# Long convolution and spectral mixing: even classes enter the modes of the middle pairs by gathered rows of U, with other room counts and an earlier last pair

## The chip, the cores and the metric

The kernel runs on one core of a Trainium2 chip. The metric is the device time of one execution in microseconds. TensorE (PE) multiplies matrices into PSUM, eight banks of 512 32-bit columns; VectorE (DVE) and ScalarE (ACT) copy results out of PSUM and work elementwise; SyncE (SP) and GpSimd (POOL) issue DMA transfers, each into a queue of its own; 16 DMA engines move the bytes.

## The reference

x is [8, 5696, 128], h is [5696, 128]. First a causal long convolution of each batch with h, by transforms of twice the length; then a mixing in the lowest 64 frequencies of the result, a residual and a small product:

```
y  = irfft(rfft(x, 2S) * rfft(h, 2S))[:, :S, :]          # S = 5696
Y  = rfft(y, S); 64 modes m:  Y2[m] = Y[m] (w_r[m] + i w_i[m])
u  = y + irfft(Y2, S)
out = u + max(u @ w_ch, 0)                               # float32
```

## The kernel before

**Stages.** S is 89 x 64, so the transform of length 2S is done in two steps. Step one (a_tile, 32 tiles) transforms over the 89 for each of 64 positions and gives 90 *classes* k = 0 to 89 (frequencies modulo 178, with their mirror images). Step two (second) transforms the 64 positions inside a class, with the twiddle factors in the strip M; the result, 64 complex frequencies as 128 partitions, lies in PSUM. It is multiplied by the filter's spectrum Hs and by its swapped copy (products), which gives U, in float16: two real factors r, two batches b, four classes of 128 channels. Two products with the constants W1 and W2 turn U back from frequencies to positions and give Z. Z goes to a scratch tensor zscr in DRAM, from which the last stage reads it with the classes on the partitions.

**Modes.** The 64 mixing modes are sums over all classes. For each class k and batch of a pair, one product with Z as the stationary operand and a slice of the constant G as the moving one adds to bank 7 (MB, lines 660 to 673): 128 columns for an odd class, but 2 or 4 for an even class, since an even class meets only the modes k/2 and 89 - k/2. At the end of a pair the sums are copied into XT (lines 696 to 699), the second copy with the sign turned.

**Pairs and ticks.** The eight batches are done as four pairs g_ (line 687). A pair has 23 ticks of four classes (NT = 23, the last of two), in three steps that overlap: tick t does second and products for its own classes, the Z products, their two copies by ScalarE and the store for tick t - 2 (LC), and the mode products for tick t - 3 (LM). Pair 0 also makes the filter's spectrum (filter_tick), whose halves are copied across partitions by SP (Hs<-Hs). While a pair runs, GpSimd loads x of the next pair (x_load, at ticks 2, 4, ... 16) and VectorE places it (x_place, ticks 9 to 22). Then comes the *border*: tiles 6 to 31 of the next pair's a_tile, four PSUM slots in turn, copied out by VectorE and ScalarE in turn. After pair 3 comes the last stage: mix multiplies the modes by the weights W, and for each 16 positions Z is loaded as ZT (load_zt, five rooms), turned into y with the constant S4, added to the mixed part (constant IB), multiplied by w_ch and stored.

**What sets the order.** The program is written out by hand: a Recorder keeps one list for each engine, in the order of the calls, and adds a semaphore wait wherever a token ("u", i), ("zs", i, b), ("bank", i) and so on was last written or read elsewhere. Each engine runs its list in order; so does each queue's issuer. A room of a buffer is a token: the writer of a room waits for all who have read it, transfers included.

**Names and lines that the prediction uses.** u_s, the U rooms: three (NU, line 229), room t % 3. z_s, the Z rooms: 6 in pair 0, 10 in pairs 1 and 2, 8 in pair 3 (NZS, line 230). products is line 586, its vector product line 607 (and 599 for the first tick); copied, the copy Xs by ScalarE that three of four products read, line 557; the Z copies and the other plain copies show as line 308 on ScalarE and 312 on VectorE, the scaled ones as 310 and 314; all matmuls are line 320, all transfers line 317. early (line 529) holds the last pair's loads by tick.

Of the kernel before, what the change touches and what calls it, by code (L numbers as in the profile page):

```python
# [4 lines left out]
P = 128  # L5
F16 = mybir.dt.float16
# [117 lines left out]
def bass_long_conv_fft__then__afno_spectral_mix_kernel(nc, x, h, moe_w_r, moe_w_i, moe_w_ch, out):  # L124
# [12 lines left out]

    qq = np.arange(NQ)
    pp = np.arange(J)
    kk = np.arange(NK)  # L140
    fwd = np.exp(-2j * np.pi * np.outer(qq, kk) / (2 * NQ))
    f1 = np.zeros((P, 2 * NK))
    f1[0:NQ] = np.stack([fwd.real, fwd.imag], axis=2).reshape(NQ, 2 * NK)
    mat = np.exp(-2j * np.pi * (pp[:, None, None] * kk[None, :, None] / L + pp[:, None, None] * pp[None, None, :] / J))
# [5 lines left out]
    th = 2.0 * np.pi * np.outer(pp, pp) / J  # L150
    c, s = np.cos(th), np.sin(th)
    w1 = np.block([[c, s], [-c, -s]])
    w2 = np.block([[-s, c], [-s, c]])
# [25 lines left out]
    for k in range(0, NK, 2):  # L179
# [2 lines left out]
        ge += [g[:, k, ri * M + m] for m in ms for ri in range(2)]  # L182
        at_e += 2 * len(ms)
    assert at_e == P
    g = np.concatenate([np.stack(ge, axis=1)] + [g[:, k] for k in range(1, NK, 2)], axis=1)

    def const(name, a):
        return nc.inline_tensor(np.ascontiguousarray(a.astype(np.float16)), name=name)
# [5 lines left out]
    c_ib = const("cIB", ib.reshape(P, -1)[:, 0:SH])  # L194
    c_sg = nc.inline_tensor(np.ascontiguousarray(sg.astype(np.float32)), name="cSG")
    c_g = const("cG", g)
    wd = nc.dram_tensor("wscr", [P, 2 * M * D], F16, kind="Internal")
    zs = nc.dram_tensor("zscr", [NP * NK * P, 2 * D], F16, kind="Internal")

# [26 lines left out]
    a_g = take(HW * 2)  # L226
    g_sb = at("G", GW, F16, a_g)
    ah_sb = at("Ah", HW, F16, a_g)
    NU, NXS, NZ, NZX = 3, 2, 6, 10
    NZS = [NZ] + [NZX] * (NP - 2) + [8]  # L230
    NZL = NZS[-1]
    a_st = take((2 * NU + NXS + NZ) * 2048)
    h_in = at("Hin", J * D, F16, a_st)
# [8 lines left out]
    u_s = [at(f"U{i}", 2048, F16, a_st + i * 4096) for i in range(NU)]  # L242
# [4 lines left out]
    wc_sb = at("Wc", 2 * P, F16, take(2 * P * 2))  # L247
    sg_sb = at("SG", 3, F32, take(12))
    XTW = 3 * M
    xt = at("XT", B * XTW, F16, a_g + GW * 2 + 2048 * (NZX - NZ))  # L250
    assert GW * 2 + 2048 * (NZX - NZ) + B * XTW * 2 <= HW * 2

    ZB = 16
    NC = 5
# [38 lines left out]
    for name, n in (("c", 16), ("x", 26), ("z", 8), ("w", 16), ("t", 10), ("s", 8), ("o", 12), ("p", 16), ("q", 10)):  # L293
        R.ring(name, n)

    def bank(i):
# [197 lines left out]
    ZY = [("zs", i, b) for i in range(NZL, NZX) for b in range(2)]  # L494
# [27 lines left out]
    def load_s4(part):  # L522
# [3 lines left out]

    V, A = "vector", "scalar"
    border = {NT - 1: [(0, 0, V)], NT: [(1, 2, V), (2, 0, V)], NT + 1: [(3, 2, A), (4, 0, V)], NT + 2: [(5, 2, V)]}
    early = {0: lambda: load_id(), 1: lambda: load_w(0), 3: lambda: load_w(1), 6: lambda: load_w(2), 8: lambda: load_w(3),
             12: lambda: load_s4(1), 16: lambda: load_s4(0),  # L530
             14: lambda: clear_zt(0),
             15: lambda: load_zt(0, "gpsimd"),
             NT - 2: lambda: (load_ib(), load_zt(1, "gpsimd", SLACK), load_zt(2, "gpsimd"), clear_zt(1), clear_zt(2))}
    pace = []
    SLACK = [("zd", NP - 1, s_) for s_ in range(NT - NZL)]

# [49 lines left out]
    def products(g_, t, sl):  # L586
        n = len(ticks[t])
        bk = [bank(sl), bank(sl + 1)]
        i = t % NU
        hv = bass.AP(h_sb, KT * t * D, [[2 * HW, P], [HW, 2], [0, 2], [1, n * D]])  # L590
        uv = bass.AP(u_s[i], 0, [[2048, P], [1024, 2], [512, 2], [1, n * D]])
        src = pv(sl, 0, [[0, 2], [512, 2], [1, n * D]])
        if t == 0:
            e = turns("e", list(range(NXS)))
            evac(bass.AP(x_s[e], 512, [[1024, P], [1, n * D]]), pv(sl + 1, 0, [[1, n * D]]), [bank(sl + 1)], [("xs", e)], eng="scalar")
            hv = bass.AP(h_sb, 0, [[2 * HW, P], [HW, 2], [1, n * D]])
            for b, s_, tok in ((0, pv(sl, 0, [[0, 2], [1, n * D]]), bank(sl)),
                               (1, bass.AP(x_s[e], 512, [[1024, P], [0, 2], [1, n * D]]), ("xs", e))):
# [8 lines left out]
        R.add("vector", lambda e: e.tensor_tensor(uv, src, hv, MULT),  # L607
              bk + [("h", t, 0), ("h", t, 1, 0), ("h", t, 1, J)], [("u", i)])

    Z_OLD = [("ag", k) for k in range(NS, NS + 8 * (NZX - NZ))]  # L610
    XPLACE = [9, 10, 12, 15, 16, 18, 20, 22], [9, 10, 13, 14, 17, 18, 20, 22]

    def zroom(g_, s_):
# [1 line left out]

    def xtok(n):
        return [("xt", n, p_) for p_ in range(2)]

    def tick(g_, t):
        if g_ + 1 < NP:  # L620
# [16 lines left out]
            a_tile(j, [sl], e)  # L637
        if g_ + 1 < NP and t % 2 == 0 and 0 < t <= 4 * XC:
            i = t // 2 - 1
            x_load(g_ + 1, i, x_st[i], xtok(i), [("u", t % NU)] + AST)  # L640
        if LC <= t < NT + LC:
            s_ = t - LC
            n = len(ticks[s_])
            i, zi = s_ % NU, zroom(g_, s_)
            zb = [turns("z", ZBANK) for b in range(2)]
            for b in range(2):
                for r in range(2):
                    mm(pv(zb[b], 0, [[1, n * D]]), (W1, W2)[r], u_s[i][:, r * 1024 + b * 512:r * 1024 + b * 512 + n * D],
                       r == 0, r == 1, [("u", i), ("wc",)], [bank(zb[b])])
                evac(bass.AP(z_s[zi], b * D, [[1024, P], [2 * D, n], [1, D]]),  # L650
                     pv(zb[b], 0, [[D, n], [1, D]]), [bank(zb[b])], [("zs", zi, b)], eng="scalar",
                     after=once(("zx", zi, b), Z_OLD) if zi >= NZ else ())
            zo = (g_ * NK + KT * s_) * P * 256
            dma("sync", bass.AP(zs, zo, [[256, P], [P * 256, n], [1, 256]]),
                bass.AP(z_s[zi], 0, [[1024, P], [256, n], [1, 256]]), "z",
                [("zs", zi, 0), ("zs", zi, 1)], [("zd", g_, s_)])
# [30 lines left out]
    for g_ in range(NP):  # L687
        for t in range(NT + LM):
# [7 lines left out]
        evac(bass.AP(xt, 2 * g_ * XTW + M, [[B * XTW, P], [XTW, 2], [1, P]]), pv(MB, 0, [[P, 2], [1, P]]),  # L696
             [bank(MB)], [("xt", g_)], 1.0 / 64, eng="scalar", after=[("ag", k) for k in range(NS + 2 * XN, NK)])
        evac(bass.AP(xt, 2 * g_ * XTW, [[B * XTW, P], [XTW, 2], [1, M]]), pv(MB, M, [[P, 2], [1, M]]),
             [bank(MB)], [("xtn", g_)], -1.0 / 64, eng="vector" if g_ + 1 == NP else "scalar", after=[("ag", k) for k in range(NS + 2 * XN, NK)])
# [197 lines left out]
```

## Time and profile before

| | |
|---|---|
| times of three runs | 392.68, 392.70, 393.31 us; median 392.7 |
| the profiled execution's own time, and its span | 392.87 us; 390.6 us |
| busy share of the span | PE 93%, PEld (weight loads) 72%, DVE 77%, ACT 80%, POOL 22% |
| to the end of pair 0's border | 0 to 109.3 us |
| pair 1: ticks, border | 109.3 to 152.0, 152.0 to 164.8 us |
| pair 2: ticks, border | 164.8 to 208.0, 208.0 to 220.9 us |
| pair 3 | 220.9 to about 262 us |
| last stage | to 390.6 us |
| chain that ended last | PE 63%, DMA 15%, DVE 8%, ACT 6% |

The profile is of one execution. Busy times count the instructions of an engine; a wait is put down to the instruction or transfer that ended it. A row of the timeline is: start, length, engine, line, operation, out<-in, and how many instructions stand in it. The window row gives for a stretch each engine's busy time and number of instructions, the granted share of TensorE's clock, the share of time in which the 16 DMA engines had packets, and the bytes moved. A transfer's time to landing runs from its issue to the last of its semaphore's updates.

### The profile page before, as it was taken

The numbers are of one execution on the slowest core, as the hardware profiler recorded it, in microseconds if no ns is written. First come the engines' busy times: TensorE is split into PE (matmuls) and PEld (weight loads), VectorE is DVE, ScalarE is ACT, GpSimd is POOL, SyncE is SP. The second block draws the span as 40 slices with busy tenths as digits, with TensorE's granted clock in tenths as the row PEclk, the third lists the DMA queues.
The fourth block names the chain that finished last, engine by engine and source line by source line (L and its number), as shares of the span: only waits on it lengthen the run. The fifth ranks groups of instructions, "written<-read, shape, count | busy, mean of one in ns | idle before, by whom it ended". The sixth has DMA issues, their size and how long they took to land.

```text
span 390.6 us, 12485 instructions
## 1 busy us (share of the span) xinstructions
PE 364.1 (93%) x5346; PEld 281.3 (72%) x5346; DVE 301.9 (77%) x346; ACT 311.2 (80%) x489; POOL 85.6 (22%) x134
## 2 busy tenths in 40 slices
PE   7799899998989999999989899989989999999992
PEld 7698766665866667856657666658878988988871
DVE  3369889987998998989998988754437767677784
ACT  8289689997989997899997899984447676777783
POOL 8600022210643210823213210319200000000000
PEclk9899999999999999999999999996999999999998
DMA  7998569998899995999995689999999999998766
GB/s 146 178 283 337 138 126 297 274 251 251 92 135 201 238 268 169 127 136 231 245 261 111 64 264 351 298 354 379 406 388 393 414 407 412 410 399 356 305 274 273
DMA packets 87090, 103.94 MB, mean 266 GB/s; under 512 B 22824, under 2 KB 72616, under 8 KB 83564
## 3 DMA queue, kind: packets, MB, share of 16 engines
q1 hardware_dynamic: 62523, 67.73, 49.7%
q0 software_dynamic: 24512, 35.43, 43.6%
q8 instruction: 42, 0.69, 0.7%
q14 instruction: 13, 0.10, 0.1%
HBM read 70.61 MB, written 51.12 MB: 312 GB/s over the span
## 4 chain that ended last, share of the span: by engine, by line
PE 63%; DMA 15%; DVE 8%; ACT 6%; issue 3%; POOL 3%; SPq 0%; POOLq 0%; DVEq 0%
PE ps L320 63%; DMA ZT4b<-zscr 4%; DMA zscr<-Zt 3%; DMA Hs<-Hs 3%; DMA Hin<-in_h_dram 3%; DMA Xt<-in_x_dram 2%; DVE As L314 2%; DVE U L599 2%; ACT As L310 2%; DVE U L607 1%; DVE Xin L361 1%; ACT UT L308 1%; ACT Zs L308 1%; DVE Hs L312 1%; ACT Xs L308 1%
## 5 line engine op out<-in xcount | busy, mean ns | idle before, releaser
L607 DVE TENSOR_TENSOR U<-Xs,Hs 128x2048 f16<-128x2048 f16 (+1 forms) x73 | 86.9, 1192 | 15.1 <-ACT Xs L308 11.0
L320 PE MATMUL ps<-U,Wc 128*128 128x512 f16 (+1 forms) x368 | 94.0, 376 | 1.3 <-DVE U L607 0.8
L308 ACT CAST Xs<-ps 128x1024 f16<-128x1024 f32 (+1 forms) x77 | 74.7, 974 | 11.9 <-PE ps L320 6.8
L308 ACT CAST Zs<-ps 128x512 f16<-128x512 f32 (+1 forms) x134 | 70.6, 595 | 2.7 <-PE ps L320 2.4
L832 DVE TENSOR_TENSOR O<-ps,R 128x512 f32<-128x512 f32 x81 | 52.5, 685 | 19.8 <-ACT R L831 12.5
L831 ACT ACTIVATE R<-ps 128x512 f32<-128x512 f32 x96 | 50.9, 572 | 16.3 <-PE ps L320 15.8
L314 DVE TENSOR_SCALAR As<-ps 128x720 f16<-128x720 f32 x70 | 57.7, 884 | 5.4 <-PE ps L320 4.8
L320 PE MATMUL ps<-F,Xin 128*128 128x180 f16 x512 | 53.7, 249 | 3.6 <-DVE Xin L361 2.3
L320 PE MATMUL ps<-As,M 64*128 64x128 f16 x1440 | 50.5, 217 | 3.5 <-DVE U L599 2.9
L320 PEld LDWEIGHTS ps<-F,Xin 128*128 128x128 f16 x512 | 44.4, 155 | 12.1 <-DVE Xin L361 2.8
L320 PE MATMUL ps<-WI,UT 128*128 128x256 f16 x360 | 51.8, 279 | 0.5 <-DVE O L832 0.4
L320 PEld LDWEIGHTS ps<-U,Wc 128*128 128x128 f16 x368 | 28.7, 97 | 30.3 <-ACT Zs L308 4.4
L310 ACT ACTIVATE As<-ps 128x720 f16<-128x720 f32 (+1 forms) x61 | 45.7, 770 | 5.7 <-PE ps L320 4.3
L317 POOL DMA_DIRECT2D Xt<-in_x_dram x48 | 26.0, 546 | 101.0 <-PE ps L320 97.1
L320 PEld LDWEIGHTS ps<-As,M 64*128 64x128 f16 x1440 | 40.6, 94 | 9.9 <-DVE U L599 3.6
L308 ACT CAST UT<-ps 128x712 f16<-128x712 f32 x40 | 30.0, 752 | 18.7 <-PE ps L320 17.7
L320 PEld LDWEIGHTS ps<-WI,UT 128*128 128x128 f16 x360 | 39.3, 152 | 4.2 <-issue 1.9
L320 PE MATMUL ps<-IBs,C 128*128 128x356 f16 x128 | 40.5, 326 | 0.6
L320 PEld LDWEIGHTS ps<-G,Zs 128*128 128x128 f16 x524 | 26.6, 96 | 14.9 <-ACT Zs L308 2.2
L607 DVE TENSOR_TENSOR U<-ps,Hs 128x2048 f16<-128x2048 f32 x15 | 34.3, 2283 | 0.0
L320 PE MATMUL ps<-G,Zs 128*128 128x128 f16 (+2 forms) x524 | 33.0, 192 | 0.1
L312 DVE CAST UT<-ps 128x712 f16<-128x712 f32 x24 | 21.4, 890 | 11.0 <-PE ps L320 11.0
(87 smaller groups left out, 509.8 us busy)
## 6 DMA issues: line engine op xcount, KB each, us to landing
out_dram<-O SPq DMA_DIRECT2D x39, 512.0 KB, 8.7
zscr<-Zs SPq DMA_DIRECT2D x64, 256.0 KB, 7.4
Xt<-in_x_dram POOLq DMA_DIRECT2D x24, 320.0 KB, 7.3
zscr<-Zt SPq DMA_DIRECT2D x24, 256.0 KB, 7.3
W<-wscr POOLq DMA_DIRECT2D x4, 1024.0 KB, 9.1
M<-cM POOLq DMA_DIRECT2D x5, 720.0 KB, 20.6
ZT0a<-zscr SPq DMA_DIRECT2D x3, 1024.0 KB, 13.1
Hs<-Hs SPq DMA_DIRECT2D x44, 64.0 KB, 6.3
```

The source lines that it names most:

```text
L308: R.add(e, lambda h_: h_.copy(dst, src), reads, writes, after=after)
L310: R.add(e, lambda h_: h_.activation(dst, src, COPY, scale=scale), reads, writes, after=after)
L312: R.add(e, lambda h_: h_.tensor_copy(dst, src), reads, writes, after=after)
L314: R.add(e, lambda h_: h_.tensor_scalar_mul(dst, src, scale), reads, writes, after=after)
L317: R.add(eng, lambda h_: h_.dma_start(dst, src), reads, writes, ring=ring, after=after)
L320: R.add("tensor", lambda h_: h_.matmul(o, l, r, start=st, stop=sp), reads, writes)
L361: R.add("vector", lambda e: e.tensor_copy(bass.AP(x_sb, i * XN * XS, [[XW, NQ], [XS, XN], [1, D]]), src), list(toks) + XZ, [("xin", i)])
L599: R.add("vector", lambda e, b=b, s_=s_: e.tensor_tensor(bass.AP(u_s[i], b * 512, [[2048, P], [1024, 2], [1, n * D]]), s_, hv, MULT), [tok, ...
L607: R.add("vector", lambda e: e.tensor_tensor(uv, src, hv, MULT), bk + [("h", t, 0), ("h", t, 1, 0), ("h", t, 1, J)], [("u", i)])
L831: R.add("scalar", lambda e: e.activation(rv, src_r, RELU), bk, [("r", i % NR)], after=once(("r", i % NR), G_ALL + XTT + [("y", 0), ("y", 1 ...
L832: R.add("vector", lambda e: e.tensor_tensor(ov, src_u, rv, ADD), bk + [("r", i % NR)], [key + (h_,)], after=once(key, old))
```

## The change

- The frequencies inside a class are put in another order: 32 and 63 change places in the strip M and in W1 and W2. With that, the frequencies that the modes of an even class need stand on partitions 0 and 64 (ticks 0 to 12) or 0, 32, 64 and 96 (ticks 13 to 22) of U.
- In pairs 1 and 2 the mode products of the even classes are left out. Instead, SP copies those partitions of each tick's U to a DRAM tensor escr, right behind the store of the tick before (even_rows: 2 or 4 partitions, of each the eight blocks of the two even classes, 128 values or 256 B a block). In the border, after tile 8, SP loads a constant cSel (66 x 512) and the 66 gathered rows of 1024 values into Z rooms 0 and 7 (even_load). After tile 27, eight products of 128 columns put their sums in a bank of the tiles' slots, VectorE adds them to XT, and ScalarE makes the copy with the sign turned from XT (even_modes). In pairs 0 and 3 the modes are made as before.
- U has four rooms in pairs 1 and 2 (three in pairs 0 and 3). Z has 6 rooms in pair 0 and 8 in the others; the fourth U room lies where two Z rooms were.
- The last pair's loads are issued at other ticks: W by ticks 0, 1, 2, 4 (before 1, 3, 6, 8), the two parts of S4 at 8 and 16 (before 12 and 16), IB at 10 (before 21).

```diff
+    jj = np.arange(J)
+    jj[[J // 2, J - 1]] = J - 1, J // 2
...
-    NU, NXS, NZ, NZX = 3, 2, 6, 10
-    NZS = [NZ] + [NZX] * (NP - 2) + [8]
+    NU, NXS, NZ, NZX, NZT = 3, 2, 6, 8, 10
+    NUS = [NU] + [NU + 1] * (NP - 2) + [NU]
+    NZS = [NZ] + [NZX] * (NP - 1)
...
-    early = {0: lambda: load_id(), 1: lambda: load_w(0), 3: lambda: load_w(1), 6: lambda: load_w(2), 8: lambda: load_w(3),
-             12: lambda: load_s4(1), 16: lambda: load_s4(0),
+    early = {0: lambda: (load_id(), load_w(0)), 1: lambda: load_w(1), 2: lambda: load_w(2), 4: lambda: load_w(3),
+             8: lambda: load_s4(1), 10: lambda: load_ib(), 16: lambda: load_s4(0),
...
-             NT - 2: lambda: (load_ib(), load_zt(1, "gpsimd", SLACK), load_zt(2, "gpsimd"), clear_zt(1), clear_zt(2))}
+             NT - 2: lambda: (load_zt(1, "gpsimd", SLACK), load_zt(2, "gpsimd"), clear_zt(1), clear_zt(2))}
...
-        i = t % NU
+        i = t % NUS[g_]
...
+    def gathers(g_):
+        return NUS[g_] > NU
+
+    def even_rows(g_, t):
+        i = t % NUS[g_]
+        p_, s_, row, to = (2, J, 4 * TB + t, TA) if t < TA else (4, J // 2, t - TA, TB)
+        dma("sync", bass.AP(es, (g_ * ER + row) * 8 * D, [[to * 8 * D, p_], [1, 8 * D]]),
+            bass.AP(u_s[i], 0, [[s_ * 2048, p_], [2 * D, 8], [1, D]]), "e", [("u", i)], [("es", g_, t)])
+
+    EZ, EC, JE = NZX - 1, 0, 27
+    EZT = [("zs", i, b) for i in (EZ, EC) for b in range(2)]
+
+    def even_load(g_):
+        dma("sync", z_s[EC][0:ER, 0:4 * P], c_sel.ap(), "e", (), [("ev", 1)], after=EZT)
+        dma("sync", z_s[EZ][0:ER, :], bass.AP(es, g_ * ER * 8 * D, [[8 * D, ER], [1, 8 * D]]), "e",
+            [("es", g_, t) for t in range(NT)], [("ev", 0)], after=EZT)
+
+    def even_modes(g_, sl):
+        for b in range(2):
+            for n in range(2):
+                for r in range(2):
+                    mm(pv(sl, b * P, [[1, P]]), z_s[EZ][0:ER, ((2 * r + b) * 2 + n) * D:((2 * r + b) * 2 + n + 1) * D],
+                       z_s[EC][0:ER, (2 * n + r) * P:(2 * n + r + 1) * P], (b, n, r) == (0, 0, 0), (b, n, r) == (1, 1, 1),
+                       [("ev", 0), ("ev", 1)] + EZT, [bank(sl)])
+        xv = bass.AP(xt, 2 * g_ * XTW + M, [[B * XTW, P], [XTW, 2], [1, P]])
+        R.add("vector", lambda e: e.tensor_tensor(xv, pv(sl, 0, [[P, 2], [1, P]]), xv, ADD), [bank(sl), ("xt", g_)], [("xt", g_)])
...
             dma("sync", bass.AP(zs, zo, [[256, P], [P * 256, n], [1, 256]]),
                 bass.AP(z_s[zi], 0, [[1024, P], [256, n], [1, 256]]), "z",
                 [("zs", zi, 0), ("zs", zi, 1)], [("zd", g_, s_)])
+            for q in range(0 if t == LC else t - 1, min(t, NT)) if gathers(g_) else ():
+                even_rows(g_, q)
...
+                    elif gathers(g_):
+                        continue
...
             for j in range(6, 32):
                 a_tile(j, [(4, 6, 0, 2)[(j - 7) % 4] if j > 6 else 0], "both" if j == 31 else V if j % 2 else A)
+                if j == 8 and gathers(g_):
+                    even_load(g_)
+                if j == JE and gathers(g_):
+                    even_modes(g_, (4, 6, 0, 2)[(j - 6) % 4])
```

More of the change, by code (lines that the diff above doesn't have):

```diff
@@ L143, in bass_long_conv_fft__then__afno_spectral_mix_kernel @@
     f1[0:NQ] = np.stack([fwd.real, fwd.imag], axis=2).reshape(NQ, 2 * NK)
-    mat = np.exp(-2j * np.pi * (pp[:, None, None] * kk[None, :, None] / L + pp[:, None, None] * pp[None, None, :] / J))
+    mat = np.exp(-2j * np.pi * (pp[:, None, None] * kk[None, :, None] / L + pp[:, None, None] * jj[None, None, :] / J))
     strip = np.stack([-mat.imag, mat.real, mat.imag], axis=2).reshape(J, NK * 3 * J)
@@ L149, in bass_long_conv_fft__then__afno_spectral_mix_kernel @@
     mt[J:P, J:MW] = strip
-    th = 2.0 * np.pi * np.outer(pp, pp) / J
+    th = 2.0 * np.pi * np.outer(jj, pp) / J
     c, s = np.cos(th), np.sin(th)
@@ L184, in bass_long_conv_fft__then__afno_spectral_mix_kernel @@
     assert at_e == P
+    TA = (2 * (NQ - M) + 2) // KT
+    TB = NT - TA
+    ER = 2 * TA + 4 * TB
+    assert TA * KT == 2 * (NQ - M) + 2
+    sel = np.zeros((ER, 2, 2, P))
+    for k in range(0, NK, 2):
+        t_, n = k // KT, k % KT // 2
+        rows_ = [(a * J, 4 * TB + a * TA + t_) for a in range(2)] if t_ < TA else \
+                [(a * J // 2, a * TB + t_ - TA) for a in range(4)]
+        for m in even[k][0]:
+            for ri in range(2):
+                for r, w in enumerate((w1, w2)):
+                    v = w @ g[:, k, ri * M + m]
+                    for r0, r1 in rows_:
+                        sel[r1, n, r, ri * M + m], v[r0] = v[r0], 0.0
+                    assert np.abs(v).max() < 1e-6
     g = np.concatenate([np.stack(ge, axis=1)] + [g[:, k] for k in range(1, NK, 2)], axis=1)
@@ L196, in bass_long_conv_fft__then__afno_spectral_mix_kernel @@
     c_g = const("cG", g)
+    c_sel = const("cSel", sel.reshape(ER, 4 * P) / 64)
+    es = nc.dram_tensor("escr", [NP * ER, 8 * D], F16, kind="Internal")
     wd = nc.dram_tensor("wscr", [P, 2 * M * D], F16, kind="Internal")
@@ L241, in bass_long_conv_fft__then__afno_spectral_mix_kernel @@
     x_st = [at(f"Xt{i}", XB, F16, a_as + i * XB * 2) for i in range(2 * XC)]
-    u_s = [at(f"U{i}", 2048, F16, a_st + i * 4096) for i in range(NU)]
+    u_s = [at(f"U{i}", 2048, F16, a_st + i * 4096) for i in range(NU)] + \
+          [at(f"U{NU}", 2048, F16, a_g + GW * 2 + (NZX - NZ) * 2048)]
     x_s = [at(f"Xs{i}", 1024, F16, a_st + NU * 4096 + i * 2048) for i in range(NXS)]
@@ L249, in bass_long_conv_fft__then__afno_spectral_mix_kernel @@
     XTW = 3 * M
-    xt = at("XT", B * XTW, F16, a_g + GW * 2 + 2048 * (NZX - NZ))
-    assert GW * 2 + 2048 * (NZX - NZ) + B * XTW * 2 <= HW * 2
+    xt = at("XT", B * XTW, F16, a_g + GW * 2 + 2048 * (NZT - NZ))
+    assert GW * 2 + 2048 * (NZT - NZ) + B * XTW * 2 <= HW * 2 and NZT - NZX == 2
     ZB = 16
@@ L292, in bass_long_conv_fft__then__afno_spectral_mix_kernel @@
     R = Recorder(nc)
-    for name, n in (("c", 16), ("x", 26), ("z", 8), ("w", 16), ("t", 10), ("s", 8), ("o", 12), ("p", 16), ("q", 10)):
+    for name, n in (("c", 16), ("x", 26), ("z", 8), ("w", 16), ("t", 10), ("s", 8), ("o", 12), ("p", 16), ("q", 10), ("e", 8)):
         R.ring(name, n)
@@ L493, in bass_long_conv_fft__then__afno_spectral_mix_kernel @@
     WT = [("w", i) for i in range(4)]
-    ZY = [("zs", i, b) for i in range(NZL, NZX) for b in range(2)]
+    ZY = [("u", NU)]
     ZX = [("zs", i, b) for i in range(NZ, NZL) for b in range(2)]
@@ L607, in products @@
         R.add("vector", lambda e: e.tensor_tensor(uv, src, hv, MULT),
-              bk + [("h", t, 0), ("h", t, 1, 0), ("h", t, 1, J)], [("u", i)])
-    Z_OLD = [("ag", k) for k in range(NS, NS + 8 * (NZX - NZ))]
+              bk + [("h", t, 0), ("h", t, 1, 0), ("h", t, 1, J)], [("u", i)], after=once(("ux", i), [("ag", k) for k in range(NK)]) if i == NU else ())
+    Z_OLD = [("ag", k) for k in range(NS, NS + 8 * (NZT - NZ))]
     XPLACE = [9, 10, 12, 15, 16, 18, 20, 22], [9, 10, 13, 14, 17, 18, 20, 22]
@@ L617, in xtok, with modes_out @@
         return [("xt", n, p_) for p_ in range(2)]
+    def gathers(g_):
[20 more added lines that the diff above has]
+        R.add("vector", lambda e: e.tensor_tensor(xv, pv(sl, 0, [[P, 2], [1, P]]), xv, ADD), [bank(sl), ("xt", g_)], [("xt", g_)])
+        evac(bass.AP(xt, 2 * g_ * XTW, [[B * XTW, P], [XTW, 2], [1, M]]),
+             bass.AP(xt, 2 * g_ * XTW + 2 * M, [[B * XTW, P], [XTW, 2], [1, M]]),
+             [("xt", g_)], [("xtn", g_)], -1.0, eng="scalar", after=[("ag", k) for k in range(NS + 2 * XN, NK)])
+    def modes_out(g_):
+        evac(bass.AP(xt, 2 * g_ * XTW + M, [[B * XTW, P], [XTW, 2], [1, P]]), pv(MB, 0, [[P, 2], [1, P]]),
+             [bank(MB)], [("xt", g_)], 1.0 / 64, eng="scalar", after=[("ag", k) for k in range(NS + 2 * XN, NK)])
+        if gathers(g_):
+            return
+        evac(bass.AP(xt, 2 * g_ * XTW, [[B * XTW, P], [XTW, 2], [1, M]]), pv(MB, M, [[P, 2], [1, M]]),
+             [bank(MB)], [("xtn", g_)], -1.0 / 64, eng="vector" if g_ + 1 == NP else "scalar", after=[("ag", k) for k in range(NS + 2 * XN, NK)])
     def tick(g_, t):
@@ L639, in tick @@
             i = t // 2 - 1
-            x_load(g_ + 1, i, x_st[i], xtok(i), [("u", t % NU)] + AST)
+            x_load(g_ + 1, i, x_st[i], xtok(i), [("u", t % NUS[g_])] + AST)
         if LC <= t < NT + LC:
@@ L643, in tick @@
             n = len(ticks[s_])
-            i, zi = s_ % NU, zroom(g_, s_)
+            i, zi = s_ % NUS[g_], zroom(g_, s_)
             zb = [turns("z", ZBANK) for b in range(2)]
@@ L695, in bass_long_conv_fft__then__afno_spectral_mix_kernel @@
                 early[t]()
[L696 to L699, printed above, removed]
+        modes_out(g_)
         if g_ + 1 < NP:
```

## The prediction

> **What bounds the kernel now.** I read, in this order, the busy time in windows, the matmul timeline, the vector engine's and the store queue's timelines, the landing times of the transfers, and the chain that ended last. The change works inside pairs 1 and 2, and pair 1 runs from 109.3 to 164.8 us. Its stretch of ticks, busy time by engine:
>
> ```profile
> core 0: us, PE busy (x) PEld busy (x) DVE busy (x) ACT busy (x) POOL busy (x), PEclk, DMA share, GB/s
> ...
> 119.00:140.00 21.00, 21.00 (x337) 13.69 (x336) 20.00 (x18) 20.57 (x34) 5.98 (x12) 1.00 1.06 238
> ```
>
> TensorE has no idle time in these 21 us, so it sets the pace, but ScalarE is free for only 0.43 us and VectorE for 1.00. The DMA share is over 1: the packets of the two queues overlap on the engines, and there is a backlog.
>
> ```profile
> 117.60 1.04 PE L320 MATMUL ps<-U,Wc 128*128 128x512 f16 x4
> 118.47 0.49 PE L320 MATMUL ps<-G,Zs 128*128 128x2 f16 x8
> 118.80 1.02 PE L320 MATMUL ps<-U,Wc 128*128 128x512 f16 x4
> 119.66 0.49 PE L320 MATMUL ps<-G,Zs 128*128 128x2 f16 x8
> 120.08 1.07 PE L320 MATMUL ps<-As,M 64*128 64x128 f16 x32
> ```
>
> Two ticks of TensorE, with the same row 3.48 us earlier (116.60) and 3.56 later (123.64): 1.76 us a tick. The eight mode products of a tick take 0.33 us (118.47 to 118.80), four odd and four even.
>
> **The saving.** Four products of 512 columns take 0.87 us (117.60 to 118.47), so 128 columns take 0.054 us and the four odd ones 0.22. The even ones keep 0.11, some 0.028 us each. A pair has 45 even classes, two products each: 90 x 0.028 = 2.5 us less; the eight new products of 128 columns cost 8 x 0.054 = 0.4. That is 2.1 us a pair, 4.2 us for two, if nothing else sets the pace. ScalarE is late next: its 0.43 us in 21.00, over the 36 us of a pair's ticks, leaves at most 0.7 us a pair.
>
> **The wait that the change adds.** A U room was free when its matmuls had read it. In pairs 1 and 2 it is now also read by the row transfer (even_rows) that SP issues right behind the store of the tick before. With four rooms, the product of tick t+4 on VectorE waits until the rows of tick t have landed. Behind that product stand, on the same in-order engine, the placing of x and the later products; behind them the Z matmuls, the Z copies, and the next store and its rows. So it closes a loop. Its lengths, for ticks 8 and 9 and the product of tick 13:
>
> ```profile
> 123.68 1.22 DVE L607 TENSOR_TENSOR U<-Xs,Hs 128x2048 f16<-128x2048 f16 x1
> ...
> 125.42 1.23 DVE L607 TENSOR_TENSOR U<-Xs,Hs 128x2048 f16<-128x2048 f16 x1
> ...
> 132.45 1.23 DVE L607 TENSOR_TENSOR U<-Xs,Hs 128x2048 f16<-128x2048 f16 x1
> ```
> ```profile
> 128.28 0.36 SPq L317 DMA_DIRECT2D zscr<-Zt  x1
> ```
>
> The product of tick 8 starts at 123.68, its store is issued at 128.28 and takes 0.36: 4.96 us until SP can issue the rows of tick 9. Those must have landed by 132.45, 3.8 us later. Over four ticks (stores at 128.28, 130.24, 131.22, 133.42; products at 123.68, 125.42, 127.37, 128.52) the first part is 4.9 us on average. So five ticks take 4.9 + L, with L from issue to landing, as soon as L is over 5 x 1.76 - 4.9 = 3.9 us.
>
> No transfer of before is as narrow as these rows (2 or 4 partitions, pieces of 256 B). The nearest are on the same queue: in this order, the stores from 116 to 142 us, the stores from 144 to 154 us, when the x loads have ended, and the 64 KB copies Hs<-Hs of pair 0 (52 to 90 us), which stand behind stores as the rows will:
>
> ```profile
> DMA to landing us min/median/max: 6.0/7.8/9.4
> ```
> ```profile
> DMA to landing us min/median/max: 1.8/3.9/5.1
> ```
> ```profile
> DMA to landing us min/median/max: 5.1/6.7/7.8
> ```
>
> A small copy behind a store lands about when the store does: the Hs copy is a quarter of a store and takes as long. So L lies between 1.8 (queue empty) and 9.4. A slower pace drains the backlog, so I take the short ends of the loaded rows: 6.0 less the 0.4 by which rows are issued after their store, and 5.1; in the middle 5.3. The pace becomes (4.9 + 5.3) / 5 = 2.04 us a tick, +0.28. It holds from tick 5, the first with a gathered room behind an x load, to about tick 20, when the last x load (issued at tick 16) is through: 15 ticks, **+4.2 us a pair**. Under this wait TensorE has idle time, and the 2.1 us saved are lost in it.
>
> The transfer engines give nearly the same. From 147 to 152 us only stores run, with a DMA share of 0.79 at 232 GB/s: 0.79 x 5.0 x 16 = 63 engine-us for 1.16 MB in pieces of 512 B, 28 ns a piece. In the loaded stretch a tick takes 1.06 x 1.76 = 1.87 us of each engine. Sixteen row pieces spread over all engines add 0.03 us to that.
> The Trainium skill (DMA: Bandwidth & Descriptors, "Why a DMA increments its semaphore by 16 and not by 1") says that a transfer uses the largest number of engines up to 16 that divides both sides' slowest dimension: 2 engines for two partitions, 4 for four. By that rule, at 28 ns a piece, 8 pieces a tick on the same engines give 1.87 + 0.22 = 2.09 us a tick, +0.33, and the sum below would be 403.2 instead of 401.7. No run here shows it yet.
>
> **The border.** even_modes stands between tiles 27 and 28 and takes bank 6, which tile 28 needs. VectorE adds 128x256 out of PSUM there; rows on both sides are 0.27 us (L832, 64x128) and 0.69 (L832, 128x512), in between 0.4. Tiles 28 and 29 can only be made after it, 0.37 us of TensorE each (149.97 to 150.34), and the border is bound by the copies out of PSUM (DVE 12.15 of 12.80 us busy). 0.4 + 0.7 = **+1.1 us a pair**; if the copies have work ahead, 0.4. The rows' load has some 9 us from the border's start to tile 27, the weight staging beside it lands in 4.5: hidden.
>
> **Nothing** for 25 more issues a pair on SP (0.36 us each, SP waits in most of a tick), nor for eight Z rooms (8 x 1.76 = 14 us against 9.4 at most).
>
> **The last pair.** W, S4 and IB are fetched sooner. Before, the end of this pair hangs on transfers:
>
> ```profile
> 250.16 11.91 DMA zscr<-Zt
> ...
> 273.48 15.12 DMA ZT4b<-zscr
> ```
> ```profile
> PE ps L320 <- DMA ZT4b<-zscr: 1.8, 1, 1.8
> ...
> ACT Zt L308 <- DMA zscr<-Zt: 1.0, 1, 1.0
> ```
>
> The IB load (734 KB, issued at 259.6, some 1.9 us at 390 GB/s) leaves this stretch, and so TensorE's wait of 1.8 us for ZT4b should go: **-1.8**, at worst 0 (W now comes in one bunch, with stores landing in up to 12 us before), at best -2.8 with ScalarE's 1.0. After it TensorE is late next.
>
> **Sum.** 392.87 us is the profiled execution's own time (span 390.6 and 2.3 around it; the median of the three runs is 392.7). 392.9 + 2 x (4.2 + 1.1) - 1.8 = **401.7 us**, 2.2% slower.
>
> **Rivals.** (1) *The rows land in time*, L under 3.9 us, because a narrow transfer passes the backlog or the few engines that it uses are ahead of the slowest. Then ScalarE limits the gain to 2 x 0.7, the borders cost 2 x 0.4 to 1.1, the end gives 1.8: 390.5 to 391.9, say **391.2**, faster. For it: the landing shown is that of the last of a store's 512 pieces, and 16 pieces may be done before; stores behind no x load land in 1.8. Against it: no Hs copy of the loaded stretch landed under 5.1.
> (2) *The pieces pile up*: if all pass through two engines, at the queue's mean packet (49.7% of 16 x 390.6 us over 62523 packets, 50 ns), 8 pieces a tick cost 0.4 us: 2.27 us a tick, +0.51 x 15 = 7.7 a pair, **408.7**. For it: the pieces are small and come from two or four partitions; against it: 28 ns for 512 B.
> (3) *TensorE alone sets the pace*, and the whole 4.2 shows: 392.9 - 4.2 + 0.8 - 1.8 = **387.7**. ScalarE's 2% speak against it.
> (4) The loop and the end cancel, because L is near 4.1: **392.9**.
>
> **Chances.** Forecast 0.60, (1) 0.16, (2) 0.17, (3) 0.03, (4) 0.04. The range, 391.0 to 411.0, takes in most of rival 1 and rival 2; some 0.1 is left below (rival 3, the lower half of rival 1) and 0.07 above (pieces over 50 ns). Among the slower cases alone it is 397 to 411. A measurement of this kernel tells 0.2% from no change: faster 0.19, same 0.04, slower 0.77.
>
> **What would show it.** U products (L607) in pairs 1 and 2 that wait for escr<-U, most of them 0.5 to 3 us, in ticks 5 to 20 and none later; TensorE with idle time before Z products; a tick of about 2.0 us until the x loads end and 1.7 after; row transfers landing in 4 to 7 us; a stall of both copy engines at tiles 28 and 29; no wait for ZT4b. Landings under 3.9 us, or U products that still wait for ScalarE alone, would make the forecast wrong; so would a granted clock that falls in the stalls, which I do not price.

## The result, and the profile after

The kernel after takes 406.64 us (median of 4 runs, 405.65 to 407.46), the kernel before 392.69 us (391.44 to 393.31) beside it: ratio 1.0409, 95% interval 1.0357 to 1.0461. The profiled execution took 405.9 us with a span of 403.3.

I cut both spans at the products U of VectorE, whose starts can be read from the timeline. "Ticks" is from the product of tick 1 to that of tick 22, "border" from there to the next pair's first product, "end" from pair 3's tick 22 to the end of the span.

| us | before | after | difference | predicted |
|---|---|---|---|---|
| to pair 1's first product | 110.0 | 109.0 | -1.0 | 0 |
| pair 1: ticks | 36.35 | 42.47 | +6.1 | +4.2 |
| pair 1: border | 17.14 | 18.61 | +1.5 | +1.1 |
| pair 2: ticks | 37.06 | 40.17 | +3.1 | +4.2 |
| pair 2: border | 17.13 | 18.60 | +1.5 | +1.1 |
| pair 3: ticks | 36.07 | 39.17 | **+3.1** | 0 |
| end | 131.07 | 129.55 | -1.5 | -1.8 |

Code that the change does not touch varies from run to run too: pair 0's ticks took 43.4 to 47.3 us in the twelve profiles below. So the experiments are read by stage, not by the total alone. The profile of experiment 8 is of an execution with a lower granted clock (0.954), so its times are not compared with the others.

From the product of tick 5 to that of tick 20, where the prediction puts the loss, pairs 1 and 2 took 27.02 us each before and 33.29 and 30.88 after. These ticks of before vary little: experiments 2 and 11, which leave pairs 1 and 2 as they were, show 27.02 us four times more. Those of the kernel after vary: experiments 1 and 9, which have the same ticks, show 32.12 and 30.87, and 32.10 and 32.19. So the loss there is 3.9 to 6.3 us a pair, and pair 1 need not lose more than pair 2.

**The ticks.** The same window as before the change, busy time and number of instructions by engine:

```profile
core 0: us, PE busy (x) PEld busy (x) DVE busy (x) ACT busy (x) POOL busy (x), PEclk, DMA share, GB/s
119.00:140.00 21.00, 17.79 (x254) 10.79 (x248) 16.81 (x14) 18.20 (x31) 5.18 (x10) 1.00 1.04 220
```

TensorE, which had no idle time, now has 3.2 us of it in 21.0. No other engine took its place: VectorE and ScalarE are idle longer too, and the granted clock is full. All engines wait, so a wait sets the pace. The waits name it (engine and tile, what ended the wait, us in total, times, longest):

```profile
PE ps L342 <- DVE U L629: 10.2, 15, 1.9
DVE U L629 <- DMA escr<-U: 8.6, 11, 1.6
...
ACT Zs L330 <- DMA zscr<-Zs: 3.4, 2, 2.5
```

VectorE's product waits for the rows of an older U, and TensorE behind it for the product. The chain of waits inside pair 1, in order of time (start, length, what):

```profile
120.82 1.14 ACT Zs L330 x2
...
121.98 0.35 SPq L339
...
122.38 6.19 DMA escr<-U
...
128.66 0.75 DVE U L629
129.41 0.39 issue
129.81 2.29 DVE U L629
...
132.11 6.09 DMA escr<-U
...
138.30 2.30 DVE U L629
...
140.65 1.17 PE ps L342 x18
...
142.32 0.60 ACT Zt L330
...
142.94 0.35 SPq L339
...
143.34 7.07 DMA escr<-U
```

Two ways through the room alternate in it. From 140.65 on the chain goes as the prediction has it: matmuls of Z, Z copies, the issue of the store (SPq), and the rows right behind it; from 120.82 it goes the same way from the copies on. Between the two it goes by row transfers and products alone. The rows of tick 6 (122.38) free the room for tick 10 (128.66); behind it the product of tick 11 ends, its rows are issued at once (132.11), and they hold the room that tick 15 needs (138.30). Products that follow a landing start 0.09 us after it. The same on VectorE's timeline, with the idle time in brackets:

```profile
128.66 1.22 DVE L629 TENSOR_TENSOR U<-Xs,Hs 128x2048 f16<-128x2048 f16 x1 [1.30 <-DMA escr<-U]
129.81 2.28 DVE L629 TENSOR_TENSOR U<-ps,Hs 128x2048 f16<-128x2048 f32 x1
133.22 1.23 DVE L629 TENSOR_TENSOR U<-Xs,Hs 128x2048 f16<-128x2048 f16 x1 [1.13 <-DMA escr<-U]
```

In ticks 5 to 18 of pair 1 the rows are issued 2.2 us after their product starts (mean) and land 5.8 us after that (in ticks 5 to 16 of pair 2: 2.5 and 5.0); from tick 20 on, with no x load in flight, they land in 1.8 us.

**The border.** Timeline of pair 1's border at the eight products:

```profile
167.26 0.61 PE L342 MATMUL ps<-Zs,Zt 66*128 66x128 f16 x8
168.38 0.41 DVE L666 TENSOR_TENSOR XT<-ps,XT 128x256 f16<-128x256 f32 x1
...
168.85 1.47 PE L342 MATMUL ps<-F,Xin 128*128 128x180 f16 x16 [0.97 <-DVE XT L666]
169.42 1.86 ACT L332 ACTIVATE As<-ps 128x720 f16<-128x720 f32 x3 [0.29 <-PE ps L342]
169.73 1.36 DVE L336 TENSOR_SCALAR As<-ps 128x720 f16<-128x720 f32 x2 [0.94 <-PE ps L342]
```

The addition takes 0.41 us, as priced. TensorE stands 0.97 us until the bank is free, and VectorE then stands 0.94 us until the next tile is there.

**The last pair.** Stores of Z while W is loaded, from the rows on zscr (ns of SP's issue min/median/max; us from issue to landing):

```profile
L339 SPq DMA_DIRECT2D zscr<-Zs x6: 360/916/4992, 238.9 to 256.0; - x6
...
DMA to landing us min/median/max: 6.2/11.9/16.4
```

In the same ticks of the kernel before these were 359/360/2007 ns and 6.2/8.4/11.6 us. And the chain in this stretch of the kernel after:

```profile
239.84 16.37 DMA zscr<-Zs
...
256.29 0.37 ACT Zs L330
```

A store of 16.4 us holds its Z room longer than eight ticks of 1.76 us last, so ScalarE's copy waits for the room. The 3.1 us of this profile are the most of all: in the seven others with the earlier loads pair 3's ticks took 37.17 to 38.31 us, and in the five with W and S4 at the old ticks 36.07 each time. The loss is 1.1 to 3.1 us.

**The end.** The granted clock falls here in every profile. The first 30 us from pair 3's tick 22, before and after:

```profile
259.60:289.60 30.00, 26.67 (x473) 22.35 (x471) 10.22 (x12) 14.05 (x20) 13.77 (x15) 0.89 1.03 384
```
```profile
273.80:303.80 30.00, 27.60 (x483) 23.37 (x481) 12.15 (x13) 14.04 (x21) 12.69 (x14) 0.83 1.02 386
```

A granted clock of 0.89 over 30 us is 3.3 us of TensorE lost, one of 0.83 is 5.1: by this estimate the kernel after lost 1.8 us more to the clock. Over all profiles the end took 126.6 to 130.7 us with the earlier loads (eight) and 129.1 to 131.1 with W and S4 as before (five), so the -1.5 of the table is no larger than what one profile differs from the next.

### The profile page after: what moved, and what is told of

Same layout as the page of the kernel before. It is cut to its first block, busy times and chain, and to the rows that moved or that the text cites. A ratio compares the mean times of both kernels' runs of the same rounds, so it can differ in the third digit from the quotient of the medians.

```text
span 403.3 us, 12184 instructions
## 1 busy us (share of the span) xinstructions
PE 362.5 (90%) x5182; PEld 276.4 (69%) x5182; DVE 304.8 (76%) x348; ACT 310.9 (77%) x489; POOL 83.9 (21%) x134
## 4 chain that ended last, share of the span: by engine, by line
PE 48%; DMA 17%; DVE 14%; ACT 11%; issue 5%; POOL 2%; SPq 0%; DVEq 0%; ACTq 0%; POOLq 0%
PE ps L342 48%; DMA escr<-U 9%; DVE As L336 6%; ACT Zs L330 4%; DMA zscr<-Zs 4%; DMA Xr<-in_x_dram 4%; DVE U L629 3%; ACT Xs L330 2%; ACT As L332 2%; DVE U L621 2%; POOL Xr L339 2%; ACT UT L330 1%; ACT R L896 1%; DVE Xin L383 1%; DVE Hs L334 1%
## 5 line engine op out<-in xcount | busy, mean ns | idle before, releaser
L330 ACT CAST Zs<-ps 128x512 f16<-128x512 f32 x150 | 81.3, 612 | 12.5 <-PE ps L342 9.1
L330 ACT CAST Xs<-ps 128x1024 f16<-128x1024 f32 (+1 forms) x77 | 75.6, 986 | 11.6 <-PE ps L342 7.1
L897 DVE TENSOR_TENSOR O<-ps,R 128x512 f32<-128x512 f32 x81 | 52.5, 684 | 20.0 <-ACT R L896 12.7
L342 PE MATMUL ps<-As,M 64*128 64x128 f16 x1440 | 51.8, 217 | 8.3 <-DVE U L629 4.6
L342 PE MATMUL ps<-G,Zs 128*128 128x2 f16 (+2 forms) x452 | 33.3, 201 | 0.1
```

What stands on the lines that cost most here:

```text
L330: R.add(e, lambda h_: h_.copy(dst, src), reads, writes, after=after)
L342: R.add("tensor", lambda h_: h_.matmul(o, l, r, start=st, stop=sp), reads, writes)
L897: R.add("vector", lambda e: e.tensor_tensor(ov, src_u, rv, ADD), bk + [("r", i % NR)], [key + (h_,)], after=once(key, old))
```

## The experiments

The theory was the prediction's: in the ticks the new reader of U's rooms is the loss, in the border the bank and the addition, in the last pair the bunch of W. The rivals: the row transfers themselves load the two or four engines that they use; the order on SP's queue; the last pair's loads gain nothing.

**1. The last pair's loads as before** (`early` of the kernel before in the kernel after: W by ticks 1, 3, 6, 8, IB at 21, S4 at 12 and 16).

> The changed kernel with the last pair's loads back at the ticks of before. Theory (the bunched weights keep the stores of pair 3 in flight until a Z room is missing): the 3.1 us that pair 3's ticks gained come back, the last stage gives up its 1.5 us: 405.0 us, and no Z copy of pair 3 waits for a store. Rival (the earlier loads are a gain that the other parts hide): 408 us.

Measured 404.89 us, median of four runs that spread too far for a ratio (398.07 to 406.63). Pair 3's ticks are back at 36.07 us, Z copies wait for a store 0.4 us in all (3.4 after), and stores land as they did before:

```profile
DMA to landing us min/median/max: 6.5/7.7/10.4
```

So pair 3's loss comes from the earlier loads. But the end took 129.11 us with the old loads, no longer than with the new ones, and TensorE did not wait for ZT4b here either: these profiles do not show that the earlier loads shorten the end. The total is too spread to tell 405.0 from 408.

**2. The last pair's loads alone** (that edit of `early` in the kernel before, and nothing else).

> The kernel before with the earlier loads of the last pair alone. Theory: +3.1 in pair 3 and -1.5 in the last stage, 394.3 us. Rival (with ten Z rooms in the pairs ahead nothing waits, the end gains): 391.2 us.

Measured 392.08 against 391.48 us, ratio 1.0017 (0.9982 to 1.0053): no difference. Pair 3's ticks +2.2 us, its end -4.4 against the profile of before. The wait is there with no gathered rows in the kernel and the old eight Z rooms of pair 3:

```profile
ACT Zs L308 <- DMA zscr<-Zs: 4.1, 4, 1.7
```

The earlier loads cost pair 3 here as they do in the kernel after, and in this profile the end gave it back. The measured 392.08 lies between the theory's number and the rival's. This end is the shortest of all, in part by the clock: over the same 30 us it was granted 0.94, which is 1.8 us of TensorE lost and not the 3.3 of before.

```profile
263.60:293.60 30.00, 29.43 (x533) 25.58 (x531) 14.22 (x16) 17.14 (x26) 13.18 (x14) 0.94 1.03 391
```

TensorE was also idle less; why is not settled.

**3. The same transfers, from a constant.** The rows come from strip M instead of U, so that no U room is held (the even classes' part of the modes of pairs 1 and 2 is then meaningless).

> The changed kernel, with the row transfers taken from the constant strip M instead of U: the same number, shape, queue and place, but U is not held (the even classes' part of the modes is then wrong). Theory (the wait for a U room is the loss): the ticks of pairs 1 and 2 take 36 us again, less at most 0.7 each; what stays is 1.5 us for each border and 1.6 for the last pair: 396 to 397.5 us. Rival (the extra pieces and issues load the transfer engines or SP): the ticks stay at 40 to 42 us, 404 to 406.6 us.

```diff
-            bass.AP(u_s[i], 0, [[s_ * 2048, p_], [2 * D, 8], [1, D]]), "e", [("u", i)], [("es", g_, t)])
+            bass.AP(m_sb, 0, [[s_ * MW, p_], [2 * D, 8], [1, D]]), "e", [("m", 0)], [("es", g_, t)])
```

Measured 396.26 us, ratio 1.0123 (1.0061 to 1.0185), as the theory had it. The ticks of the pairs fall from 42.47 and 40.17 to 35.53 and 36.18 us, while borders (18.60) and pair 3's ticks (37.76) keep theirs. The window again:

```profile
119.00:140.00 21.00, 20.69 (x292) 12.64 (x291) 19.80 (x18) 20.97 (x35) 6.22 (x12) 1.00 1.04 240
```

All the loss of the ticks is in the wait: the same pieces by the same engines cost nothing when nobody waits for them. And the row shows what the saving is worth without it: now ScalarE has no idle time (20.97 of 21.00) and TensorE has 0.31 us. Of the 2.1 us a pair that TensorE saves, 0.8 come through (ticks 1 to 20 take 33.46 us before and 32.65 here, in both pairs).

**4. The rows over more partitions** (the same number of pieces, from 16 or 32 partitions instead of 2 or 4; they carry other values of U, so the even classes' part of the modes is again meaningless).

> The changed kernel, the same number of 256 B pieces from the same U room, but from 16 or 32 partitions with one piece each, not from 2 or 4 with eight (other rows, so the even classes' part of the modes is wrong). Theory (the rows stand behind a store and wait with it): L falls by the 0.2 us that eight pieces take on one engine, and the load of the busiest engines by as much a tick: 1 to 2 us a pair back, 402 to 405 us. Rival (pieces piled on two or four engines are the loss): 397 to 398 us.

```diff
+        n_, row = (16, 2 * t) if t < TA else (32, 2 * TA + 4 * (t - TA))
+        dma("sync", bass.AP(es, (g_ * ER + row) * 8 * D, [[D, n_], [1, D]]),
+            bass.AP(u_s[i], 0, [[P // n_ * 2048, n_], [1, D]]), "e", [("u", i)], [("es", g_, t)])
```

Measured 412.76 us, ratio 1.0547 (1.0470 to 1.0624), slower than the kernel after; ticks 44.26 and 42.75. The first two row transfers of pair 1 land after 3.90 and 6.95 us, where the narrow ones took 1.88 and 2.23; but those of pair 2 take 1.92 and 2.51, as the narrow ones do there (1.77 and 2.56). In the loaded ticks the wide rows land 5.6 us (pair 1) and 5.5 us (pair 2) after their issue on average, the narrow ones 5.8 and 5.0. Both expectations missed: few partitions are not the loss, and more partitions do not make the rows land sooner. Why the ticks are longer than in the kernel after is not shown.

**5. The rows on ScalarE's queue** (`dma("scalar", ...)` in even_rows, issued in the same place).

> The changed kernel with the row transfers issued by ScalarE into its own queue; number, shape, source and the wait for U's room unchanged. Theory (a row lands late because it stands behind the store on SP's queue): it now shares the engines with the stores packet by packet and lands in 2 to 3.5 us, no U product waits for rows, the ticks of pairs 1 and 2 take 36 to 37 us: 395 to 398 us. If an issue holds ScalarE for the 0.5 us that it holds SP, ScalarE is late instead by up to 10 us a pair, with no wait for rows: 405 to 416. Rival (the engines are full, whatever the queue): rows land in 4 to 7 us and U products wait for them, 404 to 408 us.

Measured 402.05 us, ratio 1.0282 (1.0216 to 1.0347); ticks 39.38 and 38.32.

```profile
DVE U L629 <- DMA escr<-U: 3.7, 6, 1.6
```

In the kernel after this was 8.6 us in 11 waits. In most ticks the rows are issued 1.3 to 1.8 us after the product starts, but they still land 4 to 7 us later (5.2 and 5.1 on average in the two pairs). The issue comes earlier (1.7 us after the product's start on average, against 2.2 and 2.5), and that is what the ticks won; that a queue of their own would make the landing short was wrong. The time lies between the two ranges. The rival had the mechanism right: the rows land late whatever the queue, and products wait for them.

**6. The rows ahead of the store, and of the x load.** even_rows(t) is called right behind products(t), so SP issues the rows as soon as the product is done.

> The changed kernel with the rows of tick t issued in tick t, ahead of the store of tick t - 2, and not in tick t + 1 behind the store of tick t - 1. Theory (a loop of four ticks: product to issue 2.4 us, landing 5.5): the issue comes some 1 us earlier and one store fewer stands ahead, so four ticks are 1 to 1.5 us shorter until 1.76 us a tick holds again: 2 to 3 us a pair back, 400 to 403 us. Rival (load of the engines sets the pace, 2.0 us a tick): 405 to 408 us.

Measured 413.74 us, ratio 1.0518 (1.0452 to 1.0583). No U product waits for rows any more, and the kernel is slower: an x load names as its starting signal the U room of its tick (x_load with the token ("u", t % NUS)), and now the rows are recorded as readers of that room ahead of it. The rows on tile Xt in pair 1 (idle time of the issuing engine, and who waited for the loads; us, times):

```profile
  DMA escr<-U: 8.0, 2
...
who waited for it (us, times):
  DVE Xin L383: 7.5, 2
```

GpSimd holds x back until rows have landed, and VectorE's placing waits for x (14.1 us in 6 waits over the span), with the products behind it: the ticks take 44.17 and 42.78 us. The borders grow to 20.3 and 20.0 us, but there the granted clock was lower in this profile. In pair 1:

```profile
157.50:177.80 20.30, 18.40 (x191) 15.02 (x191) 15.89 (x21) 14.05 (x23) 9.16 (x13) 0.91 0.92 136
```

0.91 over 20.3 us is 1.8 us of TensorE lost, about what the border is longer than 18.6. Both expectations missed: the edit moved the wait to another queue.

**7. The rows ahead of the store, behind the x load** (the same call, later in the tick, behind x_load).

> The kernel after with the row transfer of tick t issued by SP in tick t itself, behind that tick's x load in the program's order (so the x load no longer counts the rows as readers of the room it waits for) and ahead of the store of tick t-2. Theory (the loss is that rows are issued 3 us after their product, land 4 to 7 us later and hold the U room): the rows now have 7 us from product to room, no U product waits for them, the x loads come in time, the ticks of pairs 1 and 2 fall to 35.5 to 36.5 us (42.5 and 40.2 after) and the time to 396 to 398 us. Rival (the row transfers slow the ticks wherever they are issued, as they did on ScalarE's queue): ticks of 38 to 39.5 us, 401 to 403 us. Second rival (x comes late again, as with the rows ahead of the x load): borders of 20 us, over 408 us.

Measured 400.14 us, ratio 1.0246 (1.0194 to 1.0297). The x loads are in time and the ticks fall to 38.92 and 38.63 us, not to 36. The ticks are those of the rival, the time lies between the two ranges, and the profile still names the wait for the room (2.4 us in 4 waits). The chain in pair 1:

```profile
118.67 5.19 DMA escr<-U
...
123.96 2.30 DVE U L629
...
126.28 4.93 DMA escr<-U
...
131.29 2.30 DVE U L629
...
133.61 5.25 DMA escr<-U
```

It is still the room: every fourth product reads PSUM and takes 2.30 us, its rows land 4.9 to 5.3 us after it, and the next product in the same room starts 0.09 us behind. Four ticks take 2.3 + 0.1 + 5.1 = 7.5 us, 1.87 a tick against 1.76. What failed is my "7 us from product to room": the slow product takes 2.3 of the 7.

**8. Three U rooms** in the gathered pairs instead of four.

> The changed kernel with three U rooms in pairs 1 and 2 in place of four. Theory (the loop through the room): three ticks, not four, take 2.4 + 5.5 us, 2.6 us a tick while x loads run and 1.8 to 2 after, 7 us a pair more: 418 to 422 us. Rival (load of the engines, 2.0 us a tick whatever the rooms): 406 to 409 us.

Measured 426.39 us, ratio 1.0873 (1.0786 to 1.0961). Of its profile only the order of the chain is read:

```profile
131.92 2.87 PE ps L342 x17
...
134.82 0.59 ACT Zt L330
...
135.43 0.36 SPq L339
...
135.83 3.13 DMA escr<-U
...
139.05 2.30 DVE U L629
```

It is the loop of the prediction once more: Z matmuls, Z copy, issue of the store, rows, product. The theory's sign held and its size was too small: 18 to 20 us more than the kernel after (by ratios and by medians), and not 11 to 15.

**9. The border's products after tile 31** (JE from 27 to 31, and the warming matmuls behind tile 31 into banks 2 and 3).

> The changed kernel with even_modes after tile 31 in place of tile 27, and the eight filling products that follow in banks 2 and 3. Theory (1.0 of the border's 1.5 us is the time in which tiles 28 and 29 cannot be made for want of a bank): each border takes 0.2 to 0.5 us more than before, not 1.5: 404 to 405 us. Rival (the products, the addition and the copy cost 1.5 us wherever they stand): 406 to 407 us.

Measured 406.32 us, ratio 1.0396 (1.0346 to 1.0446), the total of the kernel after; but the borders of pairs 1 and 2 took 17.42 and 17.41 us, +0.3 instead of +1.5. The addition now has no tile behind it:

```profile
174.35 0.41 DVE L666 TENSOR_TENSOR XT<-ps,XT 128x256 f16<-128x256 f32 x1
...
175.51 1.22 DVE L621 TENSOR_TENSOR U<-ps,Hs 128x1024 f16<-128x1024 f32 x1 [0.76 <-PE ps L342]
```

So the theory held for the border, and the rival's number for the total. In the profiled execution (408.12 us) pair 0 hid the gain: its ticks took 47.3 us and its border 18.72, 1.6 more than in the kernel after, with the clock at half for part of it:

```profile
97.00:101.00 4.00, 4.00 (x29) 3.01 (x27) 2.51 (x3) 1.89 (x4) 0.00 (x0) 0.57 0.66 198
```

0.57 over 4 us is 1.7 us of TensorE lost. That the other banks cost pair 0 anything is not shown; experiment 10 keeps them to the middle pairs.

**10 to 12. Putting it together.** 10: experiment 7 with the old `early` and the border's products after tile 31, the other banks in the middle pairs only. 11: the kernel before with one load moved, IB to tick 10. 12: experiment 10 with IB at tick 10.

> The same, with the last pair's loads at the ticks of the kernel before and the border's eight products after tile 31 in the middle pairs only. Theory (the terms add): pair 3's ticks 36.1 instead of 37.8 and its end 0.8 us shorter, the two borders 17.4 instead of 18.6 us each: 396.3 - 1.7 - 0.8 - 2.4 = 391.4 us, the same as the kernel before within 0.3%, since ScalarE lets only 0.8 us a pair of TensorE's saving through. Rival (the earlier loads of the last pair were needed for the end): 393 to 395. If the rows still slow the ticks: 397 to 399.

> The kernel before with one load moved: IB at tick 10 of the last pair instead of tick 21; W and S4 as before. Theory (the IB load stands in the way of ZT4b and of the last stores at the end of the pair, the bunch of W slows the ticks): ticks of pair 3 stay at 36.1 us, the wait of 1.8 us for ZT4b goes, the end is 1.8 to 4.4 us shorter: 387 to 389.7 us against 391.5. Rival (what shortened the end with all loads moved was W or S4, or only the waits that the ticks had already taken): 391 to 392 us, no difference.

> The rows behind the x load, the border's products after tile 31 and IB at tick 10, W and S4 as before. Theory (the terms add): 391.4 less what the run with IB alone gains, 387 to 389.7 us, faster than both kernels if that one is. Rival (IB gives nothing): 391 to 392.

Experiment 10: 398.07 us, ratio 1.0184 (1.0136 to 1.0232). Borders of 17.41 and 17.40 and pair 3's ticks of 36.07 us came as expected; the ticks of pairs 1 and 2 stayed at 38.24 and 39.27, and that is why the total missed 391.4 and came out in the third range, that of rows which still slow the ticks. Experiment 11: 392.88 us, ratio 1.0061 (1.0031 to 1.0091), not faster: pair 3's ticks 36.07 us, its end 130.67, and the wait stays,

```profile
PE ps L320 <- DMA ZT4b<-zscr: 1.2, 1, 1.2
```

so IB was not what ZT4b waited behind, and IB alone does not lengthen pair 3's ticks either. Where the 0.6% come from, its profile does not show. Experiment 12: 396.76 us, ratio 1.0165 (1.0114 to 1.0216). No version beats the kernel before. What is left of the loss in experiment 12 (span 394.0 against 390.6) is again the U room: ticks of 38.58 and 38.34 us, +3.5 together, and +0.5 for the borders. A fifth U room was not tried; by experiment 3, the most that it could give is 0.8 us a pair under the kernel before, against 0.3 us a pair for the border.

## Why the prediction was right, and where it was not

The forecast was 401.7 us and slower; it came to 406.6, slower, inside the range. Of the 12.7 us by which the span grew, 8.8 were forecast. The ticks of pairs 1 and 2 carry most of both numbers, by the mechanism that was named.

- **The saving hidden, ScalarE next: right.** I left at most 0.7 us a pair of TensorE's 2.1; without the wait it is 0.8 (experiment 3).
- **The U room: right mechanism, size a little low.** +6.1 and +3.1 us, together 9.2 against 8.4; the products that stand idle and start right behind a landing are those of ticks 6 to 20, and none after, as said. It is shown by taking the hold away (3) and by taking a room away (8). The loop of five ticks is in the chain, and its pace came out by luck as much as by sizing. From a product's start to the issue of the next tick's rows it is 4.4 us in pair 1 (mean of ticks 5 to 17), where I had 4.9 from ticks in which nothing waited, and the landing is 5.8, where I had 5.3: the two errors cancel, (4.4 + 5.8) / 5 = 2.04. What I left out are the 0.6 us that pass on average from a landing to the start of the product in that room, and the shorter loop that takes turns with the long one: a slow product of 2.3 us and the landing of its own rows, over four ticks. The ticks 5 to 20 took 2.22 us each in pair 1 and 2.06 in pair 2.
- **The load of the engines: wrong.** I said that it gives nearly the same; experiment 3 has the same transfers at 1.71 us a tick (13.67 us for eight). By the same run rival 2, whose 408.7 is nearest to the result in number, is wrong in its mechanism. (Rival 4's 392.9 does not follow from its own L: 4.1 gives 1.80 us a tick, +0.6 a pair, and with the borders' 1.1 some 394.5 us.)
The Trainium skill's rule on the number of engines (DMA: Bandwidth & Descriptors, "Why a DMA increments its semaphore by 16 and not by 1") agrees with the trace: a row transfer of two partitions leaves three updates of its semaphore, one of them 0.9 us after the issue and two at landing, one of four partitions five. The 2.09 us a tick that I worked out from it is near what the kernel after shows, but not for that reason: with the same transfers on the same engines and no wait, experiment 3 has 1.71, so being put on few engines cost the ticks nothing.
- **The border: right place, term too small.** 1.5 us a pair, not 1.1. I had 0.4 for the addition and 0.7 for tiles 28 and 29; VectorE alone stands 0.94 us after the 0.41. Experiments 9 and 10 take 1.2 of the 1.5 away by moving it.
- **The last pair's ticks: the step that failed.** I put "at worst 0" for the end of this pair with "W now comes in one bunch, with stores landing in up to 12 us before", and gave its ticks no term. Eight Z rooms last 14 us, as I had worked out for the other pairs, so there were 2 us of slack and a bunch that had to lengthen the landings. They came to 16.4 us, and pair 3's ticks took 3.1 us more (gone in 1, there in 2; 1.1 to 3.1 over all profiles). Whether it is the bunch of W or the earlier S4, no run tells apart; IB alone does nothing (11).
- **The end: the number is luck.** -1.5 against -1.8 and no wait for ZT4b, as said. But the end is as short with the loads as before (1), IB alone does not remove the wait (11), and the clock took 1.8 us more from the end of the kernel after than from that of before. What the earlier loads do to the end stays open.

## What to carry to other kernels

A buffer that gets a transfer as an additional reader is held for the landing, not for the copy: set (time until issue + landing time under load) against (rooms x pace), with the slowest product in the cycle, and take the landing time from the loaded stretch. Before work is taken off a full engine, look how full the next one is: here 0.8 us a pair of 2.1 could come through, and the new wait cost 3.9 to 6.3. A transfer that is brought forward is to be priced against the slack of all that is in flight where it arrives, and a call that is moved in a recorded program changes who waits on whom for every token that it reads. A stage's time in one profile is to be read with the clock granted in that stage.

## What the runs showed of the hardware that was not expected

- How many partitions a small transfer comes from changed its landing little. Sixteen or 32 pieces of 256 B landed in 5.6 and 5.5 us on average under load (ticks 5 to 18 of pair 1, 5 to 16 of pair 2) when they came from 16 or 32 partitions (experiment 4), in 5.8 and 5.0 when they came from two or four, and in 1.8 to 1.9 us in both cases in the last ticks of pair 1, when its x loads had ended.
- With transfers of other queues in flight, a small transfer takes 4 to 7 us even when its own queue holds no stores (experiment 5, ticks 5 to 18 of pair 1), and 1.7 us when the x loads have ended (ticks 21 and 22).
- SP's issue of a store, 0.36 us as a rule, took up to 4.99 us while W was loading (median 0.92 of the six Zs stores): the issue itself is held there, and with it all that stands behind it in SP's list.
- A stretch of lower granted clock shows in a stage's time: 0.91 over the 20.3 us of a border (experiment 6) and 0.57 over 4 us (experiment 9) each go with a border some 1.6 us longer.
